# Two score rounds instead of three, paired transposes, a gate in two products, rows filled ahead, spare blocks skipped, and a new order

## The chip, the cores and the metric

The kernel runs on one core of one Trainium2 chip. The metric is the device time of one execution in microseconds. TensorE (PE) multiplies matrices, VectorE (DVE), ScalarE (ACT) and GpSimd (POOL) work element by element, and SP issues most transfers. All engines run in order and wait for each other by semaphores.

## The reference

Attention with a sliding window of 128 and a linear bias, then a mixture of experts with one expert per token on top of a dense layer. B = H = 8, S = 576, head dimension 64; 4608 tokens, model width 512, 8 experts of width 512.

```python
scores = scale * np.matmul(q, k.transpose(0, 1, 3, 2))
mask = (rel >= 0) & (rel < window)
scores = np.where(mask, scores + bias[None], -1000000000.0)
attn = np.exp(scores - max); attn = attn / (sum + 1e-09)
x = (attn @ v).transpose(0, 2, 1, 3).reshape(B * S, H * D) 
y_dense = np.maximum(x @ w1_dense, 0.0) @ w2_dense
expert_idx = np.argmax(x @ w_gate, axis=1)
y_moe[mask] = gate_w[mask, None] * (np.maximum(x[mask] @ w1[e], 0.0) @ w2[e])
return y_dense + y_moe
```

## The kernel before, in words

**Units.** A unit is one batch and four heads; there are 16, two to a batch. `load_qk` brings k or q of a unit as raw rows, 18 tokens to a partition. `turn` (line 172) transposes blocks of 32 by 32 on VectorE into `ks` or `qs`, and `round_qk` (178) rounds them into `kT` or `qT` (fp32r) and puts the tokens in order: it reads contiguously and writes single elements that lie 18 elements, 72 bytes, apart. ScalarE does this 31 times and VectorE once, for the first q.

**Scores.** The 576 keys are five blocks (`kj`) of 128, the last of 64. `KP` groups them in three rounds: (0, 1), (2, 3), (4,). In each round `biases` (388) writes bias and mask into the two PSUM tiles `sq0`, `sq1` by 16 small matmuls, `scores` (414) adds the products, `expo` (431) takes the exponential of a tile into `p32`, and `low` (441) makes `plo`, the low half of a split in two bf16 numbers. The tiles exist once, so a round's biases wait for the exponentials of the round before. `attend` (455) multiplies by v in three rounds of queries, and `norm` (487) divides by the sums into `xf`. `row_copy` copies `xf` into the token rows `xrow` on GpSimd, and `flip` and `flip_copy` transpose it (`tp`, then `xT` in fp32 and `xTb` in bf16).

**Gate.** `gate_a` multiplies `xT` by the gate's weights (`lp`), `gate_av` adds the two units' halves into `ltsb`, `gate_b` turns it into `lg` by five products, `gate_bv` finds the expert of each token by five small VectorE operations from `mx` to `oh`, and `gate_c` counts them on TensorE (`pc`). `gate_cv` and `gate_d` give each token a slot (`slot`) among its expert's rows.

**Rows by expert.** `send_x` and `send_y` scatter a token's row and the dense layer's result (`dense1`: hp, hTd; `dense2`: yp, yt) to `xs_dram` and `ys_dram`, by indirect transfers on GpSimd. Then the experts' rows are worked off in 43 blocks of 128 rows (`NB`): `fetch` loads a block's rows, `turn_x`, `keep_x`, `bring`, `layer1`, `relu`, `layer2` and `gated` compute it (xps, xTm, ws, hpm, hTm, y, yo), `send_out` scatters the result. Blocks 0 to 14 (`NE`) hold only tokens of the first five batches and begin while the last batches are still in work; the others wait for all scatters. 43 is the most that any routing needs. Rows at an expert's end that no token has are filled by `late_fill` (1072): SP loads eight numbers into registers and issues sixteen transfers, which have to come after the last count and before the late blocks.

**Order.** The order on TensorE, ScalarE and VectorE is that of a program written in three tables of steps (`FIRST` for batch 0, `CYCLE` for each further batch, with how many batches late a step is, `LAST` for the end); each engine takes its instructions in that order. SP follows it too; GpSimd's own chain (`in_turn`) follows it for copies, weights and indirect transfers. After `LAST` the blocks run one like the other: two steps ahead for `turn`, `xm`, `ws`, one for `one`, `hm`.

Of the kernel before, what the change touches and what calls it, by code (L numbers as in the profile page):

```python
# [23 lines left out]
def kernel(  # L24
# [37 lines left out]
    NL = NB - NE  # L62
    RB = 32
# [137 lines left out]
    load_q(0, nc.scalar)  # L201
# [33 lines left out]
    def mask_consts():  # L235
# [28 lines left out]
    def mask_rest():  # L264
        for h in range(4, H):
            mask_head(h)

    def more_constants():
        ut_f = ident_x["ut_f"]
        nc.vector.tensor_copy(out=ut_b, in_=ut_f)  # L270
        nc.vector.memset(ones_b, 1.0)

        nc.vector.memset(sel, 0.0)
        for h in range(2):
            nc.vector.tensor_reduce(
                out=sel[64 * h : 64 * h + 64, h, :],
                in_=ident_f.rearrange("p (c x) -> p x c", c=4)[
                    64 * h : 64 * h + 64, 0:E, :
                ],
                op=ALU.add,  # L280
                axis=AX.X,
            )
# [12 lines left out]
        nc.vector.tensor_scalar_mul(out=row_f, in0=pidx_f, scalar1=float(P))
        nc.vector.memset(fill_x, 0.0)
        nc.vector.tensor_copy(out=fill_x.bitcast(I32)[:, TC : TC + 1], in_=oob_f)
# [3 lines left out]
    sel = consts.tile([P, 2, E], F32, name="sel")  # L301
# [14 lines left out]
    def pool_constants():  # L316
# [14 lines left out]
        nc.gpsimd.iota(base_i, pattern=[[ST, E]], base=0, channel_multiplier=0)  # L331
# [39 lines left out]
    lt = dbuf.tile([P, SP_ - DT[1][0] * P], F32, name="ltsb")  # L371
# [11 lines left out]
    def shape(pr):  # L383
        kjs = KP[pr]
        wid = PW if len(kjs) == 2 else TAIL
        return kjs, wid, wid * len(kjs)

    def biases(u, pr):
        hq = u % HQ
        _, _, tot = shape(pr)  # L390
# [3 lines left out]
        for rot, g in [(i, j) for i in range(4) for j in range(4)]:  # L394
            h = 4 * hq + g
            k0 = 32 * rot
            r0 = (k0 + 32 * g) % P
            if pr == 0:
                rhs = mask[r0 : r0 + 32, h, 0:PW].unsqueeze(1).to_broadcast([32, 2, PW])
            elif pr == 1:  # L400
                rhs = mask[r0 : r0 + 32, h, 0 : 2 * PW]
            else:
                rhs = mask[r0 : r0 + 32, h, 2 * PW - TAIL : 2 * PW]
            nc.tensor.matmul(
                out=sq[g // 2][k0 : k0 + 32, g % 2, 0:tot],
# [8 lines left out]
    def scores(u, pr):  # L414
        qT, kT = qkT[("q", u)], qkT[("k", u)]
        kjs, wid, _ = shape(pr)
        sq = sqs[(u, pr)]
        for i, kj in enumerate(kjs):
            nq = min(wid, S - kj * P)
            for c in range(2):  # L420
                for g in range(4):
                    nc.tensor.matmul(  # L422
                        out=sq[g // 2][:, g % 2, i * wid : i * wid + nq],
                        lhsT=kT[32 * g : 32 * g + 32, c, kj * P : kj * P + P],
                        rhs=qT[32 * g : 32 * g + 32, c, kj * P : kj * P + nq],
                        start=False,
                        stop=(c == 1 and i == len(kjs) - 1),
# [3 lines left out]
    def expo(u, pr, i):  # L431
        _, _, tot = shape(pr)
        n = 4 if pr < 2 else 2
        p32 = ppool.tile([P, 2, tot], F32, name="p32", tag=f"p32_{tot}", bufs=n)
        nc.scalar.activation(  # L435
            out=p32, in_=sqs[(u, pr)][i][:, :, 0:tot], func=ACT.Exp, scale=SCALE
        )
        phi = p32.bitcast(BF16).rearrange("p g (c t) -> p g c t", t=2)[:, :, :, 1]
        ps[(u, pr, i)] = (p32, phi)

    def low(u, pr, i):
        kjs, wid, tot = shape(pr)
        n = 4 if pr < 2 else 2
        p32, phi = ps.pop((u, pr, i))
        plo = ppool.tile([P, 2, tot], BF16, name="plo", tag=f"plo_{tot}", bufs=n)
        nc.vector.tensor_tensor(out=plo, in0=p32, in1=phi, op=ALU.subtract)  # L446
        for a, kj in enumerate(kjs):
            for x in range(2):
                pbuf[(u, kj, 2 * i + x)] = tuple(
                    t[:, x, a * wid : (a + 1) * wid] for t in (phi, plo)  # L450
                )

    cur = {}

    def attend(u, pr):
        b, hq = divmod(u, HQ)
# [30 lines left out]
    def norm(u, pr):  # L487
        b, hq = divmod(u, HQ)
        qis = KP[pr]
        rows = P if len(qis) == 2 else TAIL  # L490
        nt = len(qis)
        ax_v = cur.pop(("ax", u, pr))[:, :, 0 : 4 * (D + 1)]
        ax_v = ax_v.rearrange("p t (h d) -> p t h d", h=4)
        xf = xpool.tile([P, 2, 256], F32, name="xf", tag="xf")
        recip = gs.tile([P, 2, 4], F32, name="recip", tag="recip")
        nc.vector.reciprocal(out=recip[:rows, 0:nt], in_=ax_v[:rows, 0:nt, :, D])
        nc.vector.tensor_tensor(  # L497
            out=xf[:rows, 0:nt].rearrange("p t (h d) -> p t h d", h=4),
            in0=ax_v[:rows, 0:nt, :, 0:D],
            in1=recip[:rows, 0:nt].unsqueeze(3).to_broadcast([rows, nt, 4, D]),  # L500
            op=ALU.mult,
        )
        cur[("xf", u, pr)] = cur["xf"] = xf
# [49 lines left out]
    def gate_a(u):  # L553
        lp = psum_m.tile([P, 512], F32, name="lp", tag="misc")
        for h, (t0, t1) in enumerate(DT):
            for c in range(2):
                r0 = 64 * h + 32 * c
                nc.tensor.matmul(
                    out=lp[r0 : r0 + 32, 0:LW],
                    lhsT=wg_pad[:, 2 * (u % HQ) + c, :],  # L560
                    rhs=cur[("xT", u)][:, c, t0 * P : t0 * P + LW],
                    start=True,
                    stop=True,
                )
        gst[("lp", u)] = lp

    def gate_av(u):
        src, dst = gst.pop(("lp", u))[:, 0:LW], lt[:, 0:LW]
        if u % HQ == 0:
            nc.vector.tensor_copy(out=dst, in_=src)  # L570
        else:
            nc.vector.tensor_tensor(out=dst, in0=dst, in1=src, op=ALU.add)

    def gate_b(b):
        gst["lg"] = lg = psum_m.tile([P, NT, E], F32, name="lg", tag="misc")
        for t in range(NT):
            h = 0 if t < DT[0][1] else 1
            c0 = (t - DT[h][0]) * P
            nc.tensor.matmul(
                out=lg[:, t, :],  # L580
                lhsT=lt[:, c0 : c0 + P],
                rhs=sel[:, h, :],
# [144 lines left out]
    def dense2(b, t):  # L727
# [3 lines left out]
        yp = psum_m.tile([P, 512], F32, name="yp", tag="misc")  # L731
        for c in range(4):
            nc.tensor.matmul(  # L733
                out=yp[:rows, :],
                lhsT=cur[("hT", b, hf)][:, c, t0 * P : t0 * P + rows],
# [6 lines left out]
    def dense2_copy(b, t):  # L742
        rows = min(P, S - t * P)
        yt = xpool.tile([P, DM], F32, name="yt", tag="yt", bufs=4)
        nc.scalar.copy(out=yt[:rows, :], in_=cur.pop(("yp", b, t))[:rows, :])  # L745
        cur[("yt", b, t)] = yt

    def send_y(b, t):
# [6 lines left out]
            in_=cur.pop(("yt", b, t)).bitcast(I32)[:rows, :],  # L755
# [3 lines left out]
        in_turn(ins)  # L759

    def weights(i, after_xf):
# [47 lines left out]
        "wd": lambda b, i: weights(i, ("xf", 0, i)),  # L809
    }  # L810
# [7 lines left out]
        tk:1@-205 mask:0,0@-121 qk:0,0@-93 vl:0@-92 exp:0,0,1@-41  # L818
        exp:0,0,0@-34 lo:0,0,0@-16 mask:0,1@-8 lo:0,0,1@2 qk:0,1@5 exp:0,1,1@9
        exp:0,1,0@14 mask:0,2@14 tq:1@15 qk:0,2@15 ax:0,0@15 lo:0,1,0@17  # L820
        rq:1@18 exp:0,2,0@19 lo:0,1,1@26 norm:0,0@47 ax:0,1@50 exp:0,2,1@50
        lo:0,2,1@56 tp:0,0@58 lo:0,2,0@58 mask:1,0@59 rk:1@62 xTb:0,0@64
        xrow:0,0@64 xT:0,0@64 norm:0,1@64 qk:1,0@66 tp:0,1@66 exp:1,0,1@66
        exp:1,0,0@68 mask:1,1@69 wd:1@71 xrow:0,1@71 qk:1,1@77 ax:0,2@77
        exp:1,1,1@81 w:0@89 exp:1,1,0@89 norm:0,2@91 xrow:0,2@91 tp:0,2@91
        vl:1@95 xTb:0,1@96 xTb:0,2@98 lo:1,0,1@102 mask:1,2@102 lo:1,0,0@104
        qk:1,2@105 xT:0,2@108 exp:1,2,0@109 ax:1,0@110 xT:0,1@110 lo:1,1,0@112
        lp:0@116 lo:1,1,1@117 exp:1,2,1@117 norm:1,0@117 tp:1,0@122 xT:1,0@126
        lt:0@128 ax:1,1@128 lo:1,2,0@131 xrow:1,0@131 lo:1,2,1@136
# [518 lines left out]
```

## Time and profile before

| | us |
|---|---|
| median of 3 runs | 369.23 (366.98 to 371.61) |
| profiled execution | 369.47 |
| its span | 367.8 |
| TensorE busy | 318.5 |
| VectorE, ScalarE busy | 273.5, 272.1 |
| GpSimd busy | 223.4 |

The span is the time from the first to the last instruction on the core. Busy time is that of an engine with at least one instruction at work; matmuls overlap, so a busy TensorE need not be at its peak. A wait is idle time in front of an instruction, with what ended it.

### The profile page before, as it was taken

The page shows a single profiled execution, that of the slowest core. Times are in us where ns is not written, and L with a number is a line of the kernel's source. Part 1 is how long each engine was busy: PE and PEld are TensorE (multiplying, and loading weights), DVE is VectorE, ACT ScalarE, POOL GpSimd, SP SyncE. Part 2 cuts the span into 40 slices and gives each one's busy share as a digit, 9 for nine tenths or more (in the row PEclk, how much of TensorE's full clock was granted, in tenths as well). Part 3 has the DMA queues.
Part 4 walks back from the last instruction along what each step waited for, and adds up shares of the span by engine and source line. Part 5 has one row for each costly group of instructions (what it writes and reads, how often), then busy time and mean ns, then how long its engine had stood idle before and what let it go on. Part 6 is the DMA issues. An engine that isn't in the chain of part 4 may idle for free.

```text
span 367.8 us, 12624 instructions
## 1 busy us (share of the span) xinstructions
PE 318.5 (87%) x4972; PEld 226.9 (62%) x5003; DVE 273.5 (74%) x487; ACT 272.1 (74%) x430; POOL 223.4 (61%) x245
## 2 busy tenths in 40 slices
PE   3385888987999999999898798999999699999990
PEld 0274565665756756766665675776766467777760
DVE  7867999878799898797996978763645446676660
ACT  5778689897899999799989879876555336555640
POOL 5027612774486786488578768557777535656552
PEclk9999899998999999899999899999999879999997
DMA  7859999289569969949939995798589999989730
GB/s 199 252 132 196 187 237 234 71 234 289 141 138 276 286 131 256 262 109 303 248 107 238 242 260 129 221 255 295 169 303 317 337 303 316 316 279 307 257 123 8
DMA packets 76731, 82.43 MB, mean 224 GB/s; under 512 B 43519, under 2 KB 61311, under 8 KB 76672
## 3 DMA queue, kind: packets, MB, share of 16 engines
q1 hardware_dynamic: 58704, 47.32, 44.7%
q0 software_dynamic: 17680, 33.12, 35.7%
q10 hardware_dynamic: 288, 1.18, 0.9%
q8 instruction: 40, 0.66, 0.8%
q14 instruction: 19, 0.16, 0.1%
HBM read 64.20 MB, written 28.66 MB: 253 GB/s over the span
## 4 chain that ended last, share of the span: by engine, by line
PE 19%; POOL 14%; issue 12%; DVE 9%; ACT 2%; POOLq 1%; DMA 0%; DVEq 0%
POOL out_dram L1199 10%; DVE plo L446 4%; PE yp L733 3%; PE ax L478 3%; PE hp L706 3%; PE hpm L1156 3%; PE y L1175 2%; POOL ys_dram L750 1%; DVE xf L497 1%; POOL xs_dram L662 1%; PE tp L525 1%; DVE qs L175 1%; POOL xrow L510 1%; DVE ks L175 1%; PE xps L1121 1%
## 5 line engine op out<-in xcount | busy, mean ns | idle before, releaser
L446 DVE TENSOR_TENSOR plo<-p 128x1024 bf16<-128x1024 f32 (+1 forms) x96 | 87.1, 929 | 3.6 <-ACT p L435 3.6
L435 ACT ACTIVATE p<-sq 128x1024 f32<-128x1024 f32 (+1 forms) x96 | 74.4, 792 | 9.3 <-PE sq L422 6.8
L478 PEld LDWEIGHTS <-p 128*128 128x128 bf16 (+1 forms) x1152 | 61.9, 105 | 16.3 <-DVE xf L497 8.6
L1199 POOL DMA_INDIRECT out_dram<-yo,xr x43 | 48.4, 1125 | 37.1 <-DVE yo L1187 33.1
L510 POOL CAST xrow<-xf 128x512 bf16<-128x512 f32 (+1 forms) x48 | 47.2, 987 | 38.7 <-DVE xf L497 31.1
L478 PE MATMUL ax<-vf,p 128*128 128x65 bf16 (+1 forms) x576 | 65.2, 203 | 4.6 <-DVE xf L497 4.5
L478 PE MATMUL ax<-vf,plo 128*128 128x65 bf16 (+1 forms) x576 | 64.5, 200 | 1.1 <-DVE plo L446 1.1
L478 PE MATMUL ax<-vl,p 128*128 128x64 bf16 (+1 forms) x576 | 64.7, 199 | 0.0
L662 POOL DMA_INDIRECT xs_dram<-xrow,slot x40 | 46.0, 1150 | 29.1 <-issue 21.3
L750 POOL DMA_INDIRECT ys_dram<-yt,slot x40 | 52.5, 1313 | 15.1 <-ACT yt L745 5.4
L478 PEld LDWEIGHTS <-plo 128*128 128x128 bf16 (+1 forms) x576 | 57.7, 105 | 1.4 <-DVE plo L446 1.3
L1187 DVE SCALAR_TENSOR_TENSOR yo<-y,xr,yr 128x512 f32<-128x512 f32 x43 | 32.1, 750 | 29.1 <-PE y L1175 28.4
L1156 PE MATMUL hpm<-xTm,ws 128*128 128x128 bf16 x688 | 45.7, 221 | 1.1 <-issue 1.0
L1175 PE MATMUL y<-w_all,hTm 128*128 x156 | 43.1, 389 | 0.9
L1156 PEld LDWEIGHTS <-ws 128*128 128x128 bf16 x688 | 41.3, 99 | 3.5 <-issue 1.9
L1168 ACT ACTIVATE hTm<-hpm 128x512 bf16<-128x512 f32 x43 | 25.7, 597 | 23.7 <-PE hpm L1156 22.0
L706 PE MATMUL hp<-xTb,w_all 128*128 128x256 bf16 (+1 forms) x256 | 40.9, 289 | 1.3 <-ACT hTd L721 1.2
L733 PE MATMUL yp<-w_all,hTd 128*128 128x512 bf16 (+1 forms) x145 | 39.0, 381 | 0.7
L184 ACT CAST kT<-ks 128x1152 fp32r<-128x1152 f32 x16 | 37.9, 2370 | 1.9 <-DVE ks L175 1.8
L1130 ACT COPY xTm<-xps 128x512 bf16<-128x512 bf16 x43 | 25.1, 587 | 18.4 <-PE xps L1121 18.3
L1145 DVE COPY ws<-w_all 128x2048 bf16 x43 | 30.1, 703 | 11.3 <-PE hpm L1156 6.5
L497 DVE TENSOR_TENSOR xf<-ax,recip 128x512 f32<-128x512 f32 (+1 forms) x48 | 28.8, 600 | 12.5 <-POOL xrow L510 8.4
(126 smaller groups left out, 538.5 us busy)
## 6 DMA issues: line engine op xcount, KB each, us to landing
yr<-ys_dram SPq DMA_DIRECT2D x43, 256.0 KB
kraw<-in_k_dram SPq DMA_DIRECT2D x16, 576.0 KB
vf<-in_v_dram SPq DMA_DIRECT2D x64, 128.0 KB
w_all<-in_moe_w_dram POOLq DMA_DIRECT2D x16, 512.0 KB, 8.1
qraw<-in_q_dram SPq DMA_DIRECT2D x14, 576.0 KB
xr<-xs_dram SPq DMA_DIRECT2D x43, 130.0 KB
ys_dram<-fill_x SPq DMA_DIRECT2D x8, 256.0 KB
qraw<-in_q_dram ACTq DMA_DIRECT2D x2, 576.0 KB
```

Of the source, the lines that this page charges most:

```text
L184: copy(out=d[:, :, 0:S].rearrange("p c (x r) -> p c r x", r=R), in_=s.rearrange("p c (r x) -> p c r x", r=R),)
L435: nc.scalar.activation(out=p32, in_=sqs[(u, pr)][i][:, :, 0:tot], func=ACT.Exp, scale=SCALE)
L446: nc.vector.tensor_tensor(out=plo, in0=p32, in1=phi, op=ALU.subtract)
L478: nc.tensor.matmul(out=ax[:rows, i, o0 : o0 + w], lhsT=lhs, rhs=rhs, start=(n == 1), stop=(n == 3 * len(kl)),)
L510: ins = nc.gpsimd.tensor_copy(out=xrows[b % 2].bitcast(BF16)[:rows, qis[0] : qis[0] + nt, hq * 256 : hq * 256 + 256], in_=cur[("xf", u, pr ...
L662: ins = nc.gpsimd.indirect_dma_start(out=xs_dram[:, :], out_offset=bass.IndirectOffsetOnAxis(ap=slots[b][:rows, t : t + 1], axis=0), in_=x ...
L706: nc.tensor.matmul(out=hp[:, 0 : c1 - c0], lhsT=w_all[:, E, 0, kc, c * P : c * P + P], rhs=cur[("xTb", b)][:, kc, c0:c1], start=(kc == 0), ...
L733: nc.tensor.matmul(out=yp[:rows, :], lhsT=cur[("hT", b, hf)][:, c, t0 * P : t0 * P + rows], rhs=w_all[:, E, 1, c, :], start=(c == 0), stop ...
L750: ins = nc.gpsimd.indirect_dma_start(out=ys_dram[:, :], out_offset=bass.IndirectOffsetOnAxis(ap=slots[b][:rows, t : t + 1], axis=0), in_=c ...
L1156: nc.tensor.matmul(out=hp[:, c, :], lhsT=ws[:, kc, c * P : (c + 1) * P], rhs=xT[:, kc, :], start=(kc == 0), stop=(kc == 3),)
L1175: nc.tensor.matmul(out=y, lhsT=hT[:, c, :], rhs=w_all[:, bass.DynSlice(er, 1), 1, c, :], start=(c == 0), stop=(c == 3),)
L1199: ins = nc.gpsimd.indirect_dma_start(out=out[:, :], out_offset=bass.IndirectOffsetOnAxis(ap=xr.bitcast(I32)[:, TC : TC + 1], axis=0), in_= ...
```

## The change

It does six things. Scores go in two rounds, keys (0, 1) and (2, 3, 4); the second round fills its tile with 256, 192 and 64 columns, and for odd heads the 64 stand first, so that the tail's products serve two heads at once. The transposes write pairs of tokens side by side, and the rounding copies write pairs. The gate's `lp` is laid out by token blocks, so that `lg` needs two products. The rows to be filled lie at the front of each expert's region, which is known ahead; two large transfers (`pad`) fill them early. The last two blocks run only if the count asks for them. The three tables are new, constants move from VectorE to GpSimd, the loads of q all go through SP, `xf` has three buffers instead of two, and the first late output waits for all early ones, since a late block can repeat rows of an early one.

```diff
@@ turn, round_qk
-        nc.vector.transpose(out=s.rearrange("p c (r x) -> p r c x", r=R), in_=t)
+        nc.vector.transpose(
+            out=s.rearrange("p c (a x l) -> p a l c x", x=32, l=2),
+            in_=t.rearrange("p (a l) c x -> p a l c x", l=2),
+        )
...
-            out=d[:, :, 0:S].rearrange("p c (x r) -> p c r x", r=R),
-            in_=s.rearrange("p c (r x) -> p c r x", r=R),
+            out=d[:, :, 0:S].rearrange("p c (x a l) -> p c a x l", x=32, l=2),
+            in_=s.rearrange("p c (a x l) -> p c a x l", x=32, l=2),
@@ scores
+    KK = [(0, 1), (2, 3, 4)]
+    def part(kj, odd):
+        c0 = {0: 0, 1: PW, 2: 0, 3: PW, 4: PW + P + TAIL}[kj]
+        if odd and kj >= 2:
+            c0 = 0 if kj == 4 else c0 + TAIL
+        return c0, min(PW, S - kj * P)
@@ attend_tail, in place of 24 products of 65 columns
+            for nm, kj, x0, x1 in (
+                (4, 4, 0, 2),
+                ((3, 0), 3, 0, 1),
+                ((3, 1), 3, 1, 2),
+            ):
...
+                    nc.tensor.matmul(
+                        out=o[:, :, 0:w],
+                        lhsT=lhs,
+                        rhs=rhs,
...
@@ gate_a, gate_av, gate_b
-        for h, (t0, t1) in enumerate(DT):
-            for c in range(2):
-                r0 = 64 * h + 32 * c
+        for t, c in [(t, c) for c in range(2) for t in range(4)] + [(4, 0), (4, 1)]:
+            r0, c0, w = 32 * (t % 4), t // 4 * P, min(P, S - t * P)
...
+            if u % HQ == 0:
+                nc.scalar.copy(out=dst, in_=src)
...
-        for t in range(NT):
+        for t0, t1 in ((0, 4), (4, NT)):
@@ unused_rows (pad), in place of late_fill
+        ins = nc.sync.dma_start(
+            out=dst.rearrange("(e s) w -> s e w", e=E)[0:P],
+            in_=src.unsqueeze(1).to_broadcast([P, E, src.shape[1]]),
+        )
@@ the tables, one line of each
-        tp:1,1@1 lk:1@0 w:1@0 ax:1,2@1 xrow:1,0@1 exp:0,0,1@0 yp:0@2 xT:1,1@1
+        cv:@2 xrow:0,0@1 hp:0,3@2 lk:1@0 ex:@2 xrow:0,1@1 exp:1,1,1@1 w:0@1
@@ the end (NO = 41)
+        rest(NO, NO - 3)
+        with tc.If(reg[0] > NO - NE):
+            rest(NB)
```

What the tables do to the order is seen best in what the engines run. On VectorE, in the middle of a cycle, the gate of the batch before (from `mx` to `oh`) stood behind both transposes and two `plo`; first before, then now.

```order
L175 STREAM_TRANSPOSE ks<-kraw 128x18x2x32
L175 STREAM_TRANSPOSE qs<-qraw 128x18x2x32
L446 TENSOR_TENSOR plo<-p_3910 128x1024
L446 TENSOR_TENSOR plo<-p_3933 128x1024
L590 TENSOR_REDUCE mx<-lg 128x5
L593 TENSOR_TENSOR lgs<-lg,mx 128x40
L595 SCALAR_TENSOR_TENSOR cand<-lgs,em_133 128x40
L599 TENSOR_REDUCE e_4025<-cand 128x5
L601 TENSOR_TENSOR oh_135<-em8x,e_4025 128x40
```

```order
L198 TENSOR_TENSOR vl<-vf_155 128x1280
L632 TENSOR_TENSOR ltsb<-ltsb,lp 128x128
L632 TENSOR_TENSOR ltsb<-ltsb,lp 32x64
L176 STREAM_TRANSPOSE ks<-kraw 128x9x2x2x32
L649 TENSOR_REDUCE mx<-lg 128x5
L652 TENSOR_TENSOR lgs<-lg,mx 128x40
L654 SCALAR_TENSOR_TENSOR cand<-lgs,em_132 128x40
L658 TENSOR_REDUCE e_3641<-cand 128x5
L660 TENSOR_TENSOR oh_134<-em8x,e_3641 128x40
L442 TENSOR_TENSOR plo<-p_3607 128x1024
```

The second transpose and the two `plo` moved behind the gate. On GpSimd, where the last batch's rows are scattered (`xs_dram`, `ys_dram`) between outputs of early blocks (`out_dram`), before and now:

```order
L1199 DMA out_dram<-yo,xr 4608x512 x2
L750 DMA ys_dram<-yt,slot 37888x512
L662 DMA xs_dram<-xrow_170,slot 37888x260 x3
L750 DMA ys_dram<-yt,slot 37888x512
L662 DMA xs_dram<-xrow_170,slot 37888x260
L1199 DMA out_dram<-yo,xr 4608x512 x2
L750 DMA ys_dram<-yt,slot 37888x512
L1199 DMA out_dram<-yo,xr 4608x512
L750 DMA ys_dram<-yt,slot 37888x512
L1199 DMA out_dram<-yo,xr 4608x512
L750 DMA ys_dram<-yt,slot 37888x512
L662 DMA xs_dram<-xrow_170,slot 37888x260
```

```order
L1269 DMA out_dram<-yo,xr 4608x512
L721 DMA xs_dram<-xrow_169,slot 37888x260 x3
L1269 DMA out_dram<-yo,xr 4608x512
L812 DMA ys_dram<-yt,slot 37888x512
L1269 DMA out_dram<-yo,xr 4608x512
L812 DMA ys_dram<-yt,slot 37888x512
L721 DMA xs_dram<-xrow_169,slot 37888x260
L812 DMA ys_dram<-yt,slot 37888x512
L721 DMA xs_dram<-xrow_169,slot 37888x260
L812 DMA ys_dram<-yt,slot 37888x512
L1269 DMA out_dram<-yo,xr 4608x512 x2
L812 DMA ys_dram<-yt,slot 37888x512
```

Seven outputs stood in front of the last scatter (one of them above the rows shown), and five do now.

## Rows read from the trace of the kernel before

**Rows 1.** The page: engine busy us, share, instructions; granted clock by slice.
```profile
PE 318.5 (87%) x4972; PEld 226.9 (62%) x5003; DVE 273.5 (74%) x487; ACT 272.1 (74%) x430; POOL 223.4 (61%) x245
...
PEclk9999899998999999899999899999999879999997
```

**Rows 2.** Windows: stretch, length, busy us of each engine (instructions), clock, DMA share, GB/s.
```profile
10.70:41.80 31.10, 20.40 (x406) 16.27 (x406) 23.80 (x31) 21.82 (x27) 11.11 (x10) 0.95 0.84 193
...
67.70:218.50 150.80, 139.35 (x2471) 97.95 (x2482) 130.11 (x230) 135.99 (x211) 108.31 (x107) 0.97 0.84 212
...
289.00:298.40 9.40, 5.80 (x33) 3.60 (x33) 3.76 (x6) 1.66 (x3) 2.08 (x2) 0.64 0.97 309
```

**Rows 3.** Windows of line 435 alone, ScalarE's exponentials: busy us (instructions).
```profile
67.70:218.50 150.80, 47.22 (x60) 0.97 0.84 212
```

**Rows 4.** Windows, the stretch behind TensorE's longest wait in the cycle.
```profile
90.20:93.60 3.40, 3.40 (x50) 3.27 (x50) 2.09 (x5) 2.36 (x4) 2.18 (x2) 0.55 1.10 252
```

**Rows 5.** Timeline of TensorE: start, us, line, operation, [idle before it <- what ended that].
```profile
84.77 1.28 PE L579 MATMUL lg<-sel,ltsb 128*128 128x8 f32 x10
...
85.98 0.43 PE L404 MATMUL sq<-mask,ident 32*32 32x512 bf16 x16
...
90.17 0.30 PE L613 MATMUL pc<-oh,ones_b 128*128 128x40 bf16 x5 [2.57 <-DVE oh L601]
```

**Rows 6.** Timeline of VectorE, the same stretch.
```profile
85.44 1.38 DVE L175 STREAM_TRANSPOSE qs<-qraw 128x1152 f32<-128x1152 f32 x1 [0.94 <-DMA qraw<-in_q_dram]
...
86.75 2.32 DVE L446 TENSOR_TENSOR plo<-p 128x1024 bf16<-128x1024 f32 x2
```

**Rows 7.** Waits: who <- for whom: us in total, times, longest.
```profile
POOL xrow L510 <- DVE xf L497: 31.1, 8, 16.0
...
PE sq L404 <- ACT p L435: 9.6, 6, 2.6
...
PE pc L613 <- DVE oh L601: 7.0, 5, 2.6
```

**Rows 8.** Timeline of TensorE, a third round of scores and an lp product.
```profile
107.37 0.25 PE L404 MATMUL sq<-mask,ident 32*32 32x64 bf16 x16
...
107.55 0.72 PE L706 MATMUL hp<-xTb,w_all 128*128 128x320 bf16 x4
...
108.54 0.75 PE L558 MATMUL lp<-xT,wg_pad 128*32 128x320 f32 x8
```

**Rows 9.** Groups by line and shape: xcount | busy us, mean ns | idle before.
```profile
L184 ACT CAST kT<-ks 128x1152 fp32r<-128x1152 f32 x16 | 37.9, 2370 | 1.9 <-DVE ks L175 1.8
...
L184 DVE CAST qT<-qs 128x1152 fp32r<-128x1152 f32 x1 | 1.2, 1247 | 0.0
...
L546 ACT COPY xT<-tp 128x512 f32<-128x512 f32 x32 | 19.4, 606 | 3.5 <-PE tp L525 3.5
...
L546 ACT COPY xT<-tp 128x128 f32<-128x128 f32 x16 | 4.5, 281 | 0.9 <-PE tp L525 0.9
...
L175 DVE STREAM_TRANSPOSE ks<-kraw 128x1152 f32<-128x1152 f32 x16 | 21.9, 1368 | 3.3 <-DMA kraw<-in_k_dram 3.3
...
L446 DVE TENSOR_TENSOR plo<-p 128x128 bf16<-128x128 f32 x32 | 11.0, 351 | 1.4 <-ACT p L435 1.4
```

**Rows 10.** Timeline of TensorE, two blocks of the last stage.
```profile
349.80 1.06 PE L1156 MATMUL hpm<-xTm,ws 128*128 128x128 bf16 x16
...
351.78 1.06 PE L1156 MATMUL hpm<-xTm,ws 128*128 128x128 bf16 x16
```

**Rows 11.** Line 1134, register loads: xcount: ns min/median/max, first and last start.
```profile
L1134 PEldq TENSOR_LOAD <-erb x28: 300/358/791, 300.8 to 355.1; - x28
```

**Rows 12.** Timelines of SP's queue and of TensorE, from early to late blocks.
```profile
270.18 0.93 SPq L1082 DMA_DIRECT2D xs_dram<-fill_x  x1
...
288.54 0.37 SPq L1106 DMA_DIRECT2D xr<-xs_dram  x1
...
292.21 0.61 PE L1121 MATMUL xps<-ident,xr 128*128 128x128 bf16 x4 [3.06 <-DMA xr<-xs_dram]
```

More of the change, by code (lines that the diff above doesn't have):

```diff
@@ L905 @@
+        hm:14 yo:12 hm:13 xm:15 out:7 out:11 two:14 one:16 one:15 two:13 yo:14
+        ws:17 turn:17 yo:13 hm:15 hm:16 xm:17 two:15 out:10 out:14 out:13
+        out:12 yo:15 out:15
     """.split()
@@ L994, in table @@
         nc.vector.tensor_copy(out=er, in_=r[:, 0:1])
-        if first is None:
-            nc.vector.tensor_tensor(
-                out=ro, in0=r[:, 1:2], in1=row_f[0:RB, :], op=ALU.add
+        if early:
+            nc.vector.scalar_tensor_tensor(
+                out=ro,
+                in0=r[:, 1:2],
+                scalar=float(P),
+                in1=row_f[0:RB, :],
+                op0=ALU.add,
+                op1=ALU.add,
             )
@@ L1212, in send_out @@
         tc.add_to_no_dep_group("outs", ins.ins)
+        if j == NE:
+            for name in outs:
+                tc.add_manual_dep(
+                    ins.ins,
+                    name,
+                    mybir.DependencyInfo(
+                        mybir.DependencyClass.Sync, mybir.DependencyReason.DATA
+                    ),
+                    reason="rows of early blocks",
+                )
+        outs.append(ins.ins.name)
         in_turn(ins)
+    outs = []
     NA, NR = 5, 12
@@ L1305, with rest, count @@
         done = {x: 1 + max(k[1] for k in tail if k[0] == x) for x in ("get", *by_block)}
-        while done["get"] < done["two"] + NR:
-            fetch(done["get"])
-            done["get"] += 1
-        for j in range(done["two"], NB):
-            for x, ahead in (("turn", 2), ("xm", 2), ("ws", 2), ("one", 1), ("hm", 1)):
-                if done[x] <= j + ahead < NB:
-                    by_block[x](j + ahead)
-            for x in ("two", "yo", "out"):
-                by_block[x](j)
-            while done["get"] < min(j + NR + 1, NB):
-                fetch(done["get"])
-                done["get"] += 1
+        def rest(end, at=NB):
+            for j in range(done["two"], end):
+                if j == at:
+                    count()
+                while done["get"] < min(j + NR, end):
+                    fetch(done["get"])
+                    done["get"] += 1
+                for x, ahead in (
+                    ("turn", 2),
+                    ("xm", 2),
+                    ("ws", 2),
+                    ("one", 1),
+                    ("hm", 1),
+                    ("two", 0),
+                    ("yo", 0),
+                    ("out", 0),
+                ):
+                    while done[x] <= min(j + ahead, end - 1):
+                        by_block[x](done[x])
+                        done[x] += 1
+        reg = []
+        def count():
+            loads, (n,) = nc.values_load_multi_w_load_instructions(
+                where["n"][0:1, 0:1],
+                min_val=0,
+                max_val=NL,
+                skip_runtime_bounds_check_because="the blocks past the early ones",
+            )
+            for ins in loads:
+                if ins.ins.engine == ENG.Pool:
+                    in_turn(ins)
+            reg.append(n)
+        rest(NO, NO - 3)
+        with tc.If(reg[0] > NO - NE):
+            rest(NB)
 _INS = ['q', 'k', 'v', 'moe_w_gate', 'moe_w1_dense', 'moe_w2_dense', 'moe_w1', 'moe_w2']
```

508 lines of the change are left out of this document (265 added, 243 removed).

## The prediction, made before the changed kernel ran

> **What bounds the kernel now.** I read the page's busy shares first [rows 1]: TensorE 87%, VectorE and ScalarE 74% each. That names no bound, because it averages stages with different limits, so I cut the span with the windows view [rows 2]. The reader is to see three things there. In 10.7 to 41.8 us (batch 0) TensorE works 20.4 of 31.1 us, and no engine is full. In 67.7 to 218.5 us TensorE works 139.4 of 150.8 us, ScalarE 136.0, VectorE 130.1, and the DMA share is 0.84. Sixty exponentials start in this stretch [rows 3], six to a unit and two units to a batch, so it is five batches of 30.2 us. In 289 to 298.4 us TensorE works 5.8 of 9.4 us, and the mean granted clock is 0.64. [...] In 90.2 to 93.6 us, right after 2.6 us without a matmul, the mean clock is 0.55 [rows 4]; the page's clock line has three such dips between 67.7 and 218.5 us [rows 1].
>
> The order of instructions shows where the largest stall comes from. TensorE's queue runs lg, one mask round, one hp, one round of scores, then pc, and pc waits 2.57 us for VectorE's oh [rows 5]. VectorE had time for oh; but in front of the five gate operations its queue held a transpose of q (1.38 us) and two plo (2.32 us) [rows 6]. The waits view has this wait five times, 7.0 us in all, and another, mask rounds that wait for ScalarE's exponentials, six times, 9.6 us [rows 7].
>
> **The change, part by part**, made against the profiled execution: 369.5 us, of which 367.8 is the span; the median of the runs, 369.2, is practically the same.
>
> *Scores in two rounds.* A mask round of 64 columns starts at 107.37 and the next step at 107.55, so it takes TensorE 0.18 us [rows 8]; 16 units give -2.9 us. The 64-column score products stay. The attention products of a unit's tail become 18 instead of 24, but six of them stream twice the columns, so the columns are the same: 0. ScalarE and VectorE lose two small operations per unit each; VectorE's is 351 ns [rows 9].
>
> *Gate.* Ten passes of lg take from 84.77 to 85.98 us, 1.21 us [rows 5]; four at the same 0.121 take 0.48, and eight batches give -5.8 us. The lp product grows from 8 passes to 20. Eight take 0.75 us [rows 8]. By columns, where four column groups run side by side, 384 stand against 320: +0.15 us. By passes, at 0.094 each, it is 1.88: +1.1 us. The lg passes say that a short pass can cost as much as a long one, but each of those loads 128 columns of weights where lp's load 32. So I take the column bound, 16 x 0.15 = +2.4 us; the other end is +18. Adding up lp moves to ScalarE in half the units and lies in its new slack (below).
>
> *Spare blocks.* Blocks of the last stage follow each other in 1.98 us (349.80 to 351.78) [rows 10]. The tokens of this draw fill 41 blocks of 128 rows, so the two left out give -4.0 us. For that every engine loads a count and branches. A register load takes 0.30 to 0.79 us in that stage [rows 11]; a taken branch has no row. From below both are hidden under the last blocks; from above I allow three times the longest load, 2.4 us, all of it ahead of the last output. I take +1.
>
> TensorE's own work is down by 2.9 + 5.8 - 2.4 + 4.0 = 10.3 us, in stages where it is the bound, so this counts in full.
>
> *Order around the gate.* On VectorE the gate operations now stand behind one transpose, without the second and the two plo: 3.7 us less. On TensorE two more hp, a yp and a tail of attention stand between lg and pc. The 7.0 us of this wait should go, and with it the three dips: each a stretch of 3.4 us at half speed, 1.7 us lost, 5.1 in all. Of these 12.1 us I take 9.5, since queues that run in order turn up other waits; what is late next are VectorE's plo and xf, which now stand behind the gate.
>
> *Pairs.* The rounding casts cost 2370 ns on ScalarE for 1152 elements [rows 9]. Its copies of 512 and 128 elements, 606 and 281 ns, make 0.846 ns per contiguous element, so a contiguous cast would take 606 + 640 x 0.846 = 1147 ns. Pairs that lie 72 bytes apart, where single elements did, cost between that (all of the excess gone) and 2370 (none); paid once per jump, 1760. VectorE's one cast to the same addresses took 1247 ns [rows 9], so the addresses are not slow in themselves. I take 1250: four casts per batch relieve ScalarE of 4.5 us. That is not subtracted, since ScalarE is not the bound; it shortens the waits for exponentials.
> [...]
>
> *Head.* Mask rounds waited up to 2.6 us for ScalarE [rows 7], which had casts and three sizes of exponentials in its queue; the third round goes and the casts shorten. Against that the DMA share is 0.84 there [rows 2]. I take -4 us (0 to -7). The constants move from VectorE to GpSimd, whose first copy of rows came after 16.0 us without work [rows 7], so they cost nothing; with that cover gone, they would cost the few microseconds that they take. q's first two loads move from ScalarE's queue to SP, behind k's, and delay v's by an issue each, which nothing waits for so early.
>
> *Filling rows.* SP's queue was filling rows from 270.18 us, and only at 288.54 issued the load of the first late block; TensorE ran dry, waited 3.06 us for it [rows 12], and then went on at the lower clock [rows 2]. From 289.15, where the wait began, to 298.4 it did less than two blocks' work (4.0 us), so over 5 us were lost. Now no fill stands on SP there, and GpSimd has five outputs in front of its last scatter instead of seven. I take -4.5. The same 3.2 MB (1024 rows of 1040 and of 2048 bytes) now go through SP in batches 1 and 6, in front of loads of k, q and v. At the cycle's 212 GB/s [rows 2] they take 15 us. They are hidden while the DMA share is 0.84, and cost up to 10 us if loads come just in time. I take +2. The output of the first late block now waits until all early outputs have landed, and the later outputs queue behind it; VectorE can go on for four yo buffers, 8 us, so this costs nothing, unless a landing takes longer than that.
>
> *Sum:* 369.5 - 10.3 - 9.5 - 4 - 4.5 + 1 + 2 = 344.2, so **344 us**.
>
> **Rivals.**
> *The cast stays at 2370 ns.* For it: it also rounds to another type, and that may be its price. ScalarE keeps some 26 of 30 us per batch, so stalls return elsewhere: 5 of the 9.5 and 2 of the head's 4, 351 us.
> *Transfers become the bound.* At 0.84 the DMA engines work 25.3 us per batch, and the fills add some 2. For it: the share is over 1.0 in the stretch of [rows 4]. Against it: TensorE's long waits in the cycle name VectorE and ScalarE. The 9.5 us come back and the fills cost 4 instead of 2: 356 us.
> *lp goes by passes:* +18 instead of +2.4, 360 us.
> *Slower: the transposes.* They take 1368 ns [rows 9] and now write every second element. If that doubles them, as spreading doubled ScalarE's cast, four per batch add 5.5 us to VectorE's 26.0 [rows 2]; less 2.1 for the small operations it is 29.4, and with TensorE's present stalls of 2.3 us 31.7 per batch instead of 30.2. Seven batches lose 10.5 us, while late loads, spare blocks and branch give 7.5: 372 us. It decides from some 2.6 us per transpose. Against it: VectorE's cast to elements 72 bytes apart took 1247 ns.
> *The new order stalls as much as the old,* the head too, and loads wait in it for the fills: 9.5 + 4 + 4 more, 362 us.
>
> **How the numbers follow.** Chances: forecast 0.58 (336 to 352), cast 0.13, transfers 0.12, lp 0.06, transposes 0.05, order 0.06. The range from 333 (all waits gone, head and late loads at their best) to 358 holds the first three; the others lie above. Faster by over 2%, about what runs of this kernel can tell from no change, means under 361.8 us: 0.58 + 0.13 + 0.12 + 0.06, less a little, 0.88. Within 2%: most of order and of transposes, 0.08. Slower: 0.04.
>
> **What would show it.** Right: casts of 1150 to 1300 ns and transposes of 1368; under 2 us of waits for oh in all; lp under 0.95 us; no wait of TensorE over 1 us between early and late blocks; 41 outputs; batches of 28.5 us. Wrong: batches of 30 us, with ScalarE, VectorE or the DMA share full in them, or a new wait of TensorE behind a fill.

## The result and the profile after

The changed kernel takes 335.1 us (median of 4, 332.4 to 337.4) against 369.6 for the kernel before, measured beside it. The ratio of the two is 0.907, 95% interval 0.898 to 0.916. Here and below, runs over 1.5% longer than the fastest of the same kernel count in the median, but not in the ratio. The forecast was 344 us, range 333 to 358.

The page of the changed kernel, with the lines of [rows 1]: busy us of TensorE and its share, then the granted clock in 40 slices.

```profile
PE 295.0 (88%) x4749; PEld 217.9 (65%) x4749; DVE 257.7 (77%) x427; ACT 234.5 (70%) x411; POOL 214.4 (64%) x261
...
PEclk9999979999999999999979999999999999999996
```

The span is 333.4 us, 34.4 less than before. The windows view for the five batches (first row, as the second of [rows 2]) and for one batch in them (from one pc to the next):

```profile
61.97:194.04 132.07, 126.66 (x2342) 93.57 (x2339) 124.19 (x211) 111.69 (x198) 96.73 (x104) 0.99 1.00 256
...
105.22:130.97 25.75, 25.41 (x474) 18.83 (x471) 23.91 (x40) 22.42 (x40) 19.48 (x22) 1.00 0.99 253
```

The same for one batch of the kernel before that ran at full clock:

```profile
119.58:147.98 28.40, 27.00 (x494) 18.80 (x497) 25.36 (x44) 27.22 (x43) 21.96 (x22) 1.00 0.87 221
```

The reader is to see that even the best batch of before took 28.40 us with 1.40 idle; now it is 25.75 with 0.34 idle, and no wait of TensorE in the five batches names a transfer at the mean DMA share of 1.0. Three stretches, cut by the same events (the first exponential of unit 4 and of unit 14), show where the 34.4 us went: to unit 4 5.7 us (67.67 to 61.97), in the five batches 18.8 (150.88 to 132.07), from there to the end 9.9.

The groups of instructions that answer to [rows 9]:

```profile
L188 ACT CAST qT<-qs 128x1152 fp32r<-128x1152 f32 x16 | 20.6, 1290 | 0.0
...
L188 ACT CAST kT<-ks 128x1152 fp32r<-128x1152 f32 x16 | 20.3, 1269 | 0.5 <-DVE ks L176 0.5
...
L176 DVE STREAM_TRANSPOSE qs<-qraw 128x1152 f32<-128x1152 f32 x16 | 22.0, 1374 | 0.7 <-DMA qraw<-in_q_dram 0.4
...
L176 DVE STREAM_TRANSPOSE ks<-kraw 128x1152 f32<-128x1152 f32 x16 | 21.9, 1369 | 2.4 <-DMA kraw<-in_k_dram 2.3
```

TensorE's waits that answer to [rows 7]. The one for oh is gone; of the first two groups most lie in the head.

```profile
PE tp L582 <- DVE xf L552: 5.1, 4, 1.5
...
PE sq L419 <- ACT qT L188: 5.1, 4, 3.2
...
PE hpm L1226 <- DVE ws L1215: 3.8, 2, 1.9
...
PE sq L402 <- ACT p L430: 2.9, 3, 2.1
```

### The profile page after: what moved, and what is told of

Same layout as the page of the kernel before. It is cut to its first block, busy times and chain, and to the rows that moved or that the text cites. A ratio compares the mean times of both kernels' runs of the same rounds, so it can differ in the third digit from the quotient of the medians.

```text
span 333.4 us, 12006 instructions
## 1 busy us (share of the span) xinstructions
PE 295.0 (88%) x4749; PEld 217.9 (65%) x4749; DVE 257.7 (77%) x427; ACT 234.5 (70%) x411; POOL 214.4 (64%) x261
## 4 chain that ended last, share of the span: by engine, by line
PE 40%; DVE 15%; DMA 13%; ACT 13%; issue 8%; POOL 7%; POOLq 1%; SPq 1%; DVEq 0%; ACTq 0%
PE yp L794 7%; PE ax L533 6%; POOL out_dram L1269 6%; DMA out_dram<-yo,xr 6%; PE hp L765 5%; DVE plo L442 5%; PE sq L419 5%; ACT p L430 4%; PE tp L582 4%; PE hpm L1226 3%; DMA vf<-in_v_dram 2%; PE lp L615 2%; ACT qT L188 2%; DVE ks L176 2%; PE y L1245 2%
## 5 line engine op out<-in xcount | busy, mean ns | idle before, releaser
L442 DVE TENSOR_TENSOR plo<-p 128x1024 bf16<-128x1024 f32 x64 | 79.3, 1245 | 4.5 <-ACT p L430 3.7
L430 ACT ACTIVATE p<-sq 128x1024 f32<-128x1024 f32 x64 | 64.0, 1031 | 5.2 <-PE sq L419 3.1
L721 POOL DMA_INDIRECT xs_dram<-xrow,slot x40 | 46.0, 1149 | 19.2 <-issue 10.5
L533 PEld LDWEIGHTS <-p 128*128 128x128 bf16 x896 | 46.9, 100 | 6.6 <-DVE xf L500 3.5
L533 PE MATMUL ax<-vf,p 128*128 128x65 bf16 x448 | 47.7, 199 | 2.6 <-DVE xf L500 1.5
L533 PE MATMUL ax<-vl,p 128*128 128x64 bf16 x448 | 47.5, 195 | 0.0
L533 PE MATMUL ax<-vf,plo 128*128 128x65 bf16 x448 | 47.4, 196 | 0.1
L533 PEld LDWEIGHTS <-plo 128*128 128x128 bf16 x448 | 43.4, 99 | 0.2 <-DVE plo L442 0.2
L794 PE MATMUL yp<-w_all,hTd 128*128 128x512 bf16 x160 | 40.7, 385 | 1.4 <-ACT xT L603 0.6
L603 ACT COPY xT<-tp 128x512 f32<-128x512 f32 (+1 forms) x48 | 23.5, 489 | 17.2 <-PE tp L582 17.2
L780 ACT ACTIVATE hTd<-hp 128x256 bf16<-128x256 f32 (+1 forms) x64 | 25.0, 412 | 11.4 <-PE hp L765 10.7
```

The costliest lines, as they stand in the source:

```text
L430: nc.scalar.activation(out=p32.rearrange("p (g c) -> p g c", g=2), in_=sqs[(u, pr)][i], func=ACT.Exp, scale=SCALE,)
L533: nc.tensor.matmul(out=ax[:rows, i, o0 : o0 + w], lhsT=lhs, rhs=rhs, start=(n == 1), stop=(n == 3 * len(kl)),)
L721: ins = nc.gpsimd.indirect_dma_start(out=xs_dram[:, :], out_offset=bass.IndirectOffsetOnAxis(ap=slots[b][:rows, t : t + 1], axis=0), in_=x ...
L794: nc.tensor.matmul(out=yp, lhsT=cur[("hT", b, hf)][:, c, c0 : c0 + P], rhs=w_all[:, E, 1, c, :], start=(c == 0), stop=(c == 3),)
```

## Experiments

Each is measured beside the kernel before, on the same chip; a change of the changed kernel is compared with its ratio of 0.907 (0.898 to 0.916). The two were measured apart, though, and among the last four runs the changed kernel's own ratio was 0.942. So a difference of 0.01 is not read from ratios alone, but from rows, or from runs that were made together: the gate put back, the longer lg, the rows filled twice and the 43 blocks.

**The gate moved alone, in the kernel before.**

```diff
-        mask:1,1@0 ys:2@2 lo:1,0,0@0 ... lo:1,0,1@0 gb:@1
+        mask:1,1@0 gb:@1 ys:2@2 lo:1,0,0@0 ... lo:1,0,1@0
```

> The kernel before with one step moved in the table of the cycle: the gate's five VectorE operations (mx to oh) stand right behind the mask round that follows lg, ahead of the two plo, and behind both transposes as before. Theory (the prediction's largest term): the waits for oh, 7.0 us in five, fall under 2.5 us, the three dips of the clock that follow them go, and the time falls by 6 to 10 us, to 360 to 364. Rival (queues that run in order turn up the same stalls elsewhere): the waits for oh fall, TensorE's idle time in the five batches stays near 11.5 us, and the time stays at 367 to 371.

Measured: 378.3 us, ratio 1.024 (1.014 to 1.033): slower, by an interval that lies wholly above 1. The five batches took 157.2 us, and TensorE's idle time in them rose from 11.5 to 15.7. The waits for oh are gone altogether, but now the waits view has this in their place (4.5 us in six before):

```profile
PE ax L478 <- DVE xf L497: 15.4, 12, 2.7
```

Timelines of TensorE, then of VectorE, at the place of [rows 5, 6]:

```profile
89.55 0.28 PE L613 MATMUL pc<-oh,ones_b 128*128 128x40 bf16 x5
...
92.29 0.19 PE L478 MATMUL ax<-vf,p 128*128 128x65 bf16 x1 [1.94 <-DVE xf L497]
```

```profile
89.16 0.20 DVE L601 TENSOR_TENSOR oh<-em8x,e 128x40 bf16<-128x40 f32 x1
...
89.28 2.35 DVE L446 TENSOR_TENSOR plo<-p 128x1024 bf16<-128x1024 f32 x2
...
91.82 0.42 DVE L497 TENSOR_TENSOR xf<-ax,recip 64x256 f32<-64x256 f32 x1
```

TensorE's pc no longer waits; two steps later an attention product waits 1.94 us for the xf that stands behind the two plo. VectorE's queue is as long as it was, and TensorE needs both its oh and its xf there. The theory falls: in the order of before, where the gate stands is not what cost the time.

**Pairs alone, in the kernel before.**

```diff
-        nc.vector.transpose(out=s.rearrange("p c (r x) -> p r c x", r=R), in_=t)
+        nc.vector.transpose(
+            out=s.rearrange("p c (a x l) -> p a l c x", x=32, l=2),
+            in_=t.rearrange("p (a l) c x -> p a l c x", l=2),
+        )
```

and the cast in the same way.

> The kernel before with only the layout of the transposes and casts changed: token pairs side by side. Casts take about 1280 ns instead of 2370, transposes 1370 as before. Theory (ScalarE is not the bound, its queue only delays exponentials): 362 to 367, since part of the 9.6 us of waits of mask rounds for exponentials goes and the waits for oh stay at 7 us. Rival 1 (no engine waits long for the casts): 368 to 371. Rival 2 (the casts are what all stalls come from, also those for oh): 355 to 361, with oh waits under 3 us.

Measured: 370.7 us, ratio 1.004 (1.000 to 1.008). The casts shortened on both engines (VectorE's one from 1247 ns), and ScalarE's busy time in the five batches fell from 136.0 to 117.0 us:

```profile
L187 ACT CAST kT<-ks 128x1152 fp32r<-128x1152 f32 x16 | 20.7, 1292 | 2.0 <-DVE ks L175 2.0
...
L187 DVE CAST qT<-qs 128x1152 fp32r<-128x1152 f32 x1 | 0.8, 761 | 0.0
```

```profile
69.47:223.26 153.79, 144.26 (x2481) 100.55 (x2482) 129.61 (x230) 116.95 (x212) 111.09 (x108) 0.92 0.83 212
```

But the five batches took 153.8 us, at a mean clock of 0.92 against 0.97, and TensorE's waits fell by no more than 1.8 and 0.8 us [rows 7]:

```profile
PE sq L407 <- ACT p L438: 7.8, 6, 2.1
...
PE pc L616 <- DVE oh L604: 6.2, 4, 2.3
```

Rival 1 holds: in the order of before no engine waits long for the casts. The lower clock of the profiled run hid no gain: the six of the ten runs with a mean clock of 0.956 to 0.962 have a median of 369.6 us, and the six runs of the kernel before at 0.956 to 0.960 one of 369.7. Nor was there much for the pairs to shorten in the five batches: of the 9.6 us that mask rounds waited for exponentials before, 8.8 lie ahead of unit 4.

**Both, in the kernel before.**

> The kernel before with both: the gate moved ahead of the two plo, and token pairs. If the two gains are separate stalls they add up: 11 to 15 us less, 354 to 358. If both take away the same stalls: the larger of the two alone, within 2 us.

Measured: 377.2 us, ratio 1.015 (1.009 to 1.021). Neither expectation: the sum is a loss, as with the gate alone, with 16.1 us of waits for xf.

**The pairs undone, in the changed kernel.**

> The changed kernel with the old layout: single elements, casts of 2370 ns again. ScalarE's work in the five batches would rise from 111.7 us by 20 x 1.1 to some 133.7, which is more than the 132.1 us that they take now. Theory: ScalarE becomes the bound, 345 to 360, with waits of TensorE for exponentials and casts. The prediction's rival (only part of the stalls come back): 342. If casts are hidden behind TensorE's work all the same: under 338.

Measured: 362.3 us, ratio 0.976 (0.964 to 0.988). So some 26 of the 34 us go when only the layout goes back. The five batches, and TensorE's largest wait in the whole run (5.1 us in the changed kernel):

```profile
72.01:220.82 148.81, 127.66 (x2336) 95.15 (x2333) 124.35 (x210) 131.05 (x199) 100.84 (x102) 0.99 0.88 225
```

```profile
PE sq L416 <- ACT qT L185: 18.0, 11, 5.0
```

The five batches take 16.7 us longer at the same mean clock, nearly all of it idle time of TensorE (21.2 us against 5.4); the way to unit 4 takes 10.0 longer, and the rest no longer. The windows view of one batch, and TensorE's longer waits in it:

```profile
121.86:151.48 29.62, 25.61 (x470) 19.12 (x470) 24.03 (x39) 26.28 (x41) 20.01 (x22) 1.00 0.84 215
```

```profile
127.35 0.70 PE L762 MATMUL hp<-xTb,w_all 128*128 128x320 bf16 x4 [1.03 <-ACT yt L804]
...
136.96 1.02 PE L791 MATMUL yp<-w_all,hTd 128*128 128x512 bf16 x4 [0.66 <-ACT hTd L777]
...
142.46 0.74 PE L416 MATMUL sq<-qT,kT 32*128 32x256 f32 x16 [1.23 <-ACT qT L185]
...
151.48 0.27 PE L669 MATMUL pc<-oh,ones_b 128*128 128x40 bf16 x5 [0.77 <-ACT hTd L777]
```

All four wait for ScalarE, 3.7 us together, and the batch is 29.62 us, 3.87 longer. ScalarE is not full (26.3 of 29.6): the queues wait for each other in turn, as ScalarE at 144.93 us does for TensorE's attention products, 1.65 us. So ScalarE is the cause without being 100% busy. The theory's direction holds; the time is 2 us above its range, and of the waits that it named, those for casts came and those for exponentials did not (2.6 us, against 2.9 in the changed kernel).

**The gate put back, in the changed kernel.**

```diff
-        gb:@1 hp:0,0@1 ... qk:1,1@0 lo:1,0,0@0 ys:2@2
+        hp:0,0@1 ... qk:1,1@0 lo:1,0,0@0 gb:@1 ys:2@2
```

> The changed kernel with the gate's five VectorE operations put back in the table of the cycle, behind two plo and one xf. Theory (where the gate stands on VectorE decides): oh comes about 3.3 us later (two plo of 1.2, xf with its reciprocal 0.9), waits of TensorE for oh of 1 to 2.5 us in each of six batches, and lower clock behind them: 343 to 350. Rival (the work that now stands between lg and pc on TensorE hides it): 334 to 338, waits for oh under 2 us in all.

Measured: 340.0 us, ratio 0.921 (0.919 to 0.923), 4 us above the run with rows filled twice, made beside it (336.0), and between the two expectations. TensorE's idle time in the five batches rose from 5.4 to 10.5 us, at full clock. Its waits between 60 and 230 us:

```profile
PE hp L765 <- ACT hTd L780: 4.1, 5, 0.8
...
PE pc L672 <- DVE oh L660: 0.4, 1, 0.4
```

The work between lg and pc does hide a late oh, as the rival said (0.4 us); the price appears as waits of hp for ScalarE's hTd, which the changed kernel didn't have there. So in the new order the gate's place is worth some 4 us, by another wait than the one predicted.

**Longer lg, in the changed kernel.**

```diff
-        for t0, t1 in ((0, 4), (4, NT)):
+        for t0, t1 in ((0, 4), (4, NT)) + 3 * ((4, NT),):
```

> The changed kernel with three repeats of the gate's last product, so that lg takes ten passes again instead of four (same values written again). Six passes of some 0.11 to 0.12 us in each of eight batches are 5.3 to 5.8 us of TensorE. Theory (TensorE is the bound and its work counts in full): 340 to 341. Rival (VectorE, 94% busy in the five batches now, or the transfers, share 1.00, are the bound): under 337.

Measured: 339.0 us, ratio 0.919 (0.916 to 0.922). One batch:

```profile
107.97:134.31 26.34, 25.74 (x475) 19.47 (x477) 23.96 (x40) 22.43 (x40) 19.33 (x22) 1.00 0.94 237
```

This batch is 0.59 us longer, the next 0.71 (26.45 against 25.74), of some 0.7 added. By the batches TensorE's work counts nearly in full, though VectorE is busy 24 of 26.3 us. The median lies 1 us under the theory's range and 2 above the rival's.

**Filling rows twice, in the changed kernel.**

```diff
         apart(nm, b, ins)
+        nc.sync.dma_start(
+            out=junk[i].rearrange("(e s) w -> s e w", e=E)[0:P],
+            in_=src.unsqueeze(1).to_broadcast([P, E, src.shape[1]]),
+        )
```

> The changed kernel with each of the two transfers that fill rows issued a second time, into memory that nothing reads: 3.2 MB more through SP's queue at the same places. Theory (transfers hidden, the fill costs nothing or the 2 us that I took): 334 to 338. Rival (transfers are the bound at a share of 1.00): 3.2 MB at the 256 GB/s of the five batches are 12 us more, 345 to 349.

Measured: 336.0 us, ratio 0.912 (0.907 to 0.918), span 333.3 against 333.4. The intervals overlap: 3.2 MB more cost nothing that shows, where the rival asked for 12 us. Transfers are not the bound at a share of 1.0. That the first fill costs nothing either is argued from the second; it was not taken out.

**All 43 blocks, in the changed kernel.**

```diff
-        rest(NO, NO - 3)
-        with tc.If(reg[0] > NO - NE):
-            rest(NB)
+        rest(NB)
```

> The changed kernel with all 43 blocks run without a condition, no count and no branch. Theory (two blocks of 1.98 us less about 1 us for count and branch): 3 us more, 337 to 339.5. Rival 1 (count and branch cost as much as the blocks): 335 or less. Rival 2 (they cost nothing): 339 to 340.

Measured: 340.7 us (338.4 to 344.4), ratio 0.921 (0.917 to 0.925), above all three ranges. The median is 5.7 above that of the changed kernel and 4.7 above the run with rows filled twice, made beside it; the profiled spans differ by 3.3 (336.7 against 333.4). So leaving out the two blocks gains 3 to 6 us, and how much of that is theirs the times don't tell. The rows settle the branch's price: from the start of the last block's first layer to the start of the last output, without the branch and with it.

```profile
324.64 1.06 PE L1226 MATMUL hpm<-xTm,ws 128*128 128x128 bf16 x16
...
328.91 0.98 POOL L1269 DMA_INDIRECT out_dram<-yo,xr  x1 [0.30 <-issue]
```

```profile
320.29 1.05 PE L1226 MATMUL hpm<-xTm,ws 128*128 128x128 bf16 x16
...
325.78 0.98 POOL L1269 DMA_INDIRECT out_dram<-yo,xr  x1 [1.53 <-DMA out_dram<-yo,xr]
```

That is 4.27 us against 5.49: count and branch cost 1.2 us, against two blocks of 1.98. The difference is the last row's wait (1.53 us against 0.30): at the line of the branch GpSimd's queue spends 1.58 us waiting for an earlier output to land.

**Work moved on TensorE, in the kernel before.** The last four runs were on another chip than the other experiments, and all took longer: the kernel before 392.2 us and the changed kernel as it is 369.9, ratio 0.942 (0.931 to 0.953). The casts last as long there (1270 to 1291 ns). In the profile of the changed kernel there, TensorE has some 6 us of idle time, in 15 waits, with no releaser that the profile shows, where its first profile had 0.2 in one. These stand in front of passes of lp:

```profile
PE lp L615 <- issue: 1.9, 5, 0.5
```

That is a part of the 35 us at most; what is late there stays open. These four are compared only with each other and with the kernel before on that chip.

```diff
-        ys:4@2 lo:1,0,1@0 gb:@1
+        ys:4@2 lo:1,0,1@0 hp:0,1@1 hTd:0,0@1 hp:0,2@1 hTd:0,1@1 gb:@1
```

(each of the four is taken out where it stood).

> The kernel before with work moved on TensorE instead of on VectorE: two hp products (0.6 us each, with the ScalarE steps that follow them) that stood behind pc in the cycle now stand between the scores and pc; VectorE's order is as before. It stems from the run with the gate moved alone, where the waits for oh went to zero and waits of the attention products for xf of 2 to 2.7 us took their place. Theory (TensorE lacked work there, and what stands in the stretch decides, not where the gate stands): waits for oh under 3 us in all, no new wait of 2 us in the cycle, 360 to 365. Rival (the products moved leave the same hole further on, where they stood): 367 to 372.

Measured: 395.3 us, ratio 1.012 (1.003 to 1.021): no gain. The waits for oh are gone, and so are waits over 0.6 us in the middle batches, at full clock; yet one takes 29.31 us:

```profile
123.07:152.38 29.31, 27.33 (x494) 19.12 (x496) 25.54 (x43) 26.92 (x44) 20.01 (x20) 1.00 0.82 204
```

```profile
123.96 0.63 PE L525 MATMUL tp<-ident_f,xf 128*128 128x128 f32 x4 [0.58 <-DVE basee L640]
...
127.03 0.75 PE L558 MATMUL lp<-xT,wg_pad 128*32 128x320 f32 x8 [0.52 <-ACT xTb L546]
```

The theory falls, and the rows speak for the rival: the idle time, 1.98 us in this batch, is spread over small waits, such as these two behind pc, where the products had stood. There is no profile of the kernel before on this chip to set beside them.

> The same with the token pairs, casts of 1280 ns. Theory (the shorter casts are worth something once TensorE's order has no hole): 4 us or more under the run without pairs. Rival (ScalarE is not waited for in the order of before, whatever TensorE's is): within 2 us of the run without pairs.

Measured: 397.1 us, ratio 1.017 (1.007 to 1.027): within 2 us of the run without pairs. Again the rival.

**Two small repairs of the changed kernel.**

```diff
-        round_qk(0, "q")
+        round_qk(0, "q", nc.vector.tensor_copy)
...
-        yo = mpool.tile([P, DM], F32, name="yo", tag="yo", bufs=4)
+        yo = mpool.tile([P, DM], F32, name="yo", tag="yo", bufs=6)
```

> The changed kernel with six yo buffers instead of four, and the first cast of q on VectorE, beside ScalarE's of k. Theory: the wait of 1.9 us at the first late blocks (yo waits 2.7 us for an early output to land) goes, and the first scores start about 1 us sooner: 2 to 3 us less than the changed kernel of the same call. Rival (what waits for the landing only waits at another place; the head's next wait takes up the microsecond): no difference beyond 1 us.

> The changed kernel as it is, for comparison with the one before it in this call: 332 to 338, as measured.

Measured: 366.8 us with the repairs and 369.9 without, ratios 0.941 (0.930 to 0.951) and 0.942 (0.931 to 0.953). The first exponential starts at 10.38 instead of 11.44 us, as expected; whether the whole gains can't be told. The other repair had nothing to remove: on this chip the kernel as it is shows no wait of yo for an output to land. The run as it is missed its expectation of 332 to 338, by what was said above.

## Why the prediction was right, and where it was not

The direction and the sign of every stage came out, and 335.1 us lies in the range; the forecast was 9 us too high. The mechanism given to its largest single term was wrong, and a term that it put at nothing, the pairs, turned out to carry most of the gain. That the total still fell into the range is in part luck.

**TensorE's work** was the bound, as said, but its saving was sized at half. By my terms it was 0.79 us per batch. Windows of single lines give lg, mask rounds, scores and lp in one batch, before and then after (first busy time):

```profile
119.58:147.98 28.40, 1.28 (x10) 1.19 (x10) 1.00 0.87 221
...
119.58:147.98 28.40, 2.24 (x96) 0.83 (x96) 1.00 0.87 221
...
119.58:147.98 28.40, 3.73 (x80) 2.76 (x80) 1.00 0.87 221
...
119.58:147.98 28.40, 1.49 (x16) 0.31 (x16) 1.00 0.87 221
```

```profile
105.22:130.97 25.75, 0.59 (x4) 0.53 (x4) 1.00 0.99 253
...
105.22:130.97 25.75, 1.75 (x64) 0.65 (x64) 1.00 0.99 253
...
105.22:130.97 25.75, 3.24 (x84) 2.62 (x80) 1.00 0.99 253
...
105.22:130.97 25.75, 1.69 (x40) 1.37 (x40) 1.00 0.99 253
```

lg 0.69 less (0.73 expected), masks 0.49 (0.36), lp 0.20 more (0.30), all near. What failed is "the 64-column score products stay": scores took 0.49 less. The products did stay, but not their time. In a round of their own the eight passes took 0.41 us; in the joint round they add 0.14 to the 0.74 of the other sixteen. The two rounds before, then the joint one:

```profile
122.06 0.41 PE L422 MATMUL sq<-qT,kT 32*128 32x64 f32 x8
...
126.82 0.74 PE L422 MATMUL sq<-qT,kT 32*128 32x256 f32 x16
```

```profile
117.22 0.88 PE L419 MATMUL sq<-qT,kT 32*128 32x256 f32 x24
```

With smaller shares elsewhere TensorE's busy time fell by 1.59 us per batch, and in five batches by 8.0 instead of 3.9. That lp costs its columns and not its passes was the right choice between the two bounds.

**Order around the gate: 9.5 of 12.1 us.** The size came near by luck; the reason was wrong. By the two windows above, five batches at the pace of before's best one are 142.0 us of its 150.9, so 8.9 were stalls and low clock; now 3.3 remain of 132.1. Idle time at full clock fell by another 1.06 per batch. That makes 5.6 + 5.3 = 10.9 us. (With the work it is 18.9 of the 18.8 measured, as it must be: both are cut from the same rows.) The three dips are in the trace of before as the 5.1 us take them: a granted clock of 0.50 for 3.4 us each, from 89.8, 147.8 and 209.2 us on. The five batches of the changed kernel have one, from 171.4. But I derived the 9.5 from where five VectorE operations stand. Moving them alone made the kernel before slower, and filling TensorE's hole alone did not help either. The step that failed is "what are late next are VectorE's plo and xf": named, and then priced within 2.6 us, when in the kernel before they took the whole gain and more. In the new order the gate's place is worth some 4 us, by the run that put it back. What else in the new tables brings the gain, apart from the pairs, was not separated: the tables of before have other steps.

**Pairs.** Casts of 1269 to 1290 ns (1250 expected) and transposes of 1369 to 1374 (1368). "ScalarE is not the bound" was right for the kernel before, where pairs gain nothing. It was wrong to carry it to the new order, and to the rival in it: with casts of 2370 ns I gave 351 us, and it was 362. Without the pairs the five batches took 148.8 us, only 2.1 less than before, so of the 18.8 gained there 16.7 hang on the pairs. ScalarE's work did not have to reach 100% of a batch; by the waits, the new order had no slack for it. My reading that "the addresses are not slow in themselves", as VectorE's cast took 1247 ns, was wrong too: with pairs it took 761.
The casts shortened on both engines (ScalarE's from 2370 to 1280 ns, VectorE's from 1247 to 761), while ScalarE's 1280 stays above the 1147 estimated from its contiguous copies; those read PSUM and do not round, and which of this makes the difference was not tested. Why a cast to pairs is shorter than one to single elements was not shown either.

**Filling rows.** The 2 us for transfers were not there. The late loads are: the wait of 3.06 us for xr [rows 12] is gone, and so is the clock of 0.50 that followed it, from 291.2 to 298.1 us. But "no wait of TensorE over 1 us" between early and late blocks did not come out. GpSimd's outputs, then VectorE, then TensorE, at the first late blocks:

```profile
266.49 1.49 POOL L1269 DMA_INDIRECT out_dram<-yo,xr  x1 [0.88 <-DVE yo L1257]
...
274.95 1.18 POOL L1269 DMA_INDIRECT out_dram<-yo,xr  x1 [2.43 <-DVE yo L1257]
```

```profile
273.92 0.75 DVE L1257 SCALAR_TENSOR_TENSOR yo<-y,xr,yr 128x512 f32<-128x512 f32 x1 [2.67 <-DMA out_dram<-yo,xr]
...
275.67 0.55 PE L1226 MATMUL hpm<-xTm,ws 128*128 128x128 bf16 x7 [1.91 <-DVE ws L1215]
```

The first late block's yo takes the buffer of the output four before it. That one started at 266.49 and had landed only when yo started, 7.4 us later; TensorE waited 1.91 us. So the four buffers were too few, but not by what I had feared: the first late output, which has to wait for the early ones, starts at 274.95, 0.28 us behind its yo. Even so the stretch from unit 14 to the end gave 9.9 us, against the 8.3 of its terms (4.0 + 4.5 - 1 and one batch of work).

**Head, branch and the other signs.** To unit 4 5.7 us, against 5.6 from the head's 4 and two batches of work; but with the pairs undone that way took 72.0 us, more than before, so the head's gain hangs on the pairs as well, where the rival left it half. Count and branch 1.2 (1 expected). Waits for oh under 2 us, 41 outputs and lp under 0.95 us came out. "Batches of 28.5 us" did not, and it did not follow from my own terms either: 18.8 - 7.4 = 11.4 us in five batches are 27.9. Of the 9 us that the forecast was too high, 7.4 are from there (4.1 of work, 2 of fills, 1.4 of stalls, rounded) and 1.6 from the late stage. In the rival on the transposes, the 2.1 us for small operations are 1.4 by the row that I gave (four of 351 ns); it would have said 377 us instead of 372.

## What to carry to other kernels

A wait in the profile names the last link of a chain of in-order queues. If the same engine has as much queued for the next step, moving the waited-for operation only moves the wait (here 7.0 us for oh went, and waits for xf rose from 4.5 to 15.4), so ask what the waiting engine needs within the next few microseconds, and price that. An edit that gains nothing alone (shorter casts, ratio 1.004) can carry most of the gain of another (a tighter order, 26 of 34 us): test each by undoing it in the changed kernel, not only by adding it to the old one. When TensorE is the bound, take the best batch at full clock as the measure of its work, and count stalls and clock against that.

## What was not expected of the hardware

A mean DMA share of 1.0 in the five batches left TensorE unhindered, and 3.2 MB more changed the span by 0.1 us. The pairs sped up VectorE too: its cast of the first q fell from 1247 to 761 ns, though its 1247 had looked fast beside ScalarE's 2370. In the last runs, on another chip, both kernels took 23 to 35 us more with casts as long as before, and the gain was 5.8% instead of 9.3%. The ratio of one set of runs did not hold in another, and why is open.
